# The last three bits of each converted weight: a GpSimd multiply-add in place of a ScalarE instruction

## The chip, the cores and the metric

One core of a Trainium2 chip. The metric is the device time of one execution in microseconds (us). Engines are named as the profile names them: PE is TensorE (matrix products; PEld its weight loads), DVE is VectorE, ACT is ScalarE, POOL is GpSimd, SP issues the DMAs.

## The reference

Attention with a memory, then two feed-forward blocks. The activations are float32; the feed-forward weights reach the device as 64-bit floats.

```python
scores = scale * q @ k.T                      # B, H, S, D = 4, 8, 576, 64; causal
a = softmax(scores); local = a @ v
mem_out = (phi(q) @ M_prev) / (phi(q) @ z_prev + 1e-06)
x = g * mem_out + (1 - g) * local             # -> [2304, 512]
x = ((x @ w1) * (x @ w2)) @ w3 @ w_out        # 512 -> 1024 -> 1024 -> 512
out = (sigmoid(x @ w_gate) * (x @ w_val)) @ w_out2   # 512 -> 1536 -> 512
```

## The kernel before

The kernel goes through the four batches in turn. While batch b is in its feed-forward part (`ffn`), the attention of batch b+1 is woven into it (`drive`, from line 1045). The time up to some 106 us is different: there the attention of batch 0 runs beside the preparation of a combined weight (w3 times w_out, `prep`, line 552; its products are the wps products of line 464). Attention works on four pairs of heads and, in each, on five row blocks of 116. For a pair p, a block i and a head hh of the pair the tile `p_<p>_<i>_<hh>` holds the scores. They go through TensorE (line 838, tile s), VectorE (line 843: mask, row maximum), ScalarE (line 119: exponential), VectorE (lines 866 and 867: reciprocal of the row sum), GpSimd or VectorE (line 869: scaling; in batch 0 always GpSimd), TensorE (line 899: transposes, tile t), and on to the products with the values (tile o). The memory part of a pair has two products that GpSimd may do (lines 781, tile me, and 790, tile mphi).

Every weight is a 64-bit float in memory. It is converted to a 32-bit float on the device, in halves of a unit of 128x512 numbers, 76 halves in all; `conv_step` does this. `load64` (line 282) brings a raw half of 512 KB into one of three buffers (tile r). Step 0 makes two tiles: cy on ScalarE (line 310) from the upper words, and cr (line 311) from the lower words, a whole number from 0 to 7 for the last three bits; both have two buffers. Behind step 0 the load of the half three places later is issued, and it waits until both instructions have read the buffer. Step 1 joins them on VectorE (line 319: cy shifted left by three, or cr) into the tile wraw. Then `split_step` splits the 32-bit number into two parts for TensorE's products: a cast on ScalarE (line 548) and a subtraction on VectorE (line 550) into the tile wo or wslot, which has five buffers. The function `pump` calls a conversion step and a split step between groups of products; while weights are missing, `prep` calls them directly.

The order on the engines: SP's opening and, from the first feed-forward on, TensorE's whole order are as the code writes them. All other orders are worked out when the kernel is built, by a scheduler that places each instruction by its own estimates of times and by priorities (the attention of batch 0 has a higher one). On the chip every engine goes through its list in that order, and an instruction that waits holds up all that stand behind it on its engine.

Of the kernel before, what the change touches and what calls it, by code (L numbers as in the profile page):

```python
# [10 lines left out]
U32 = mybir.dt.uint32  # L11
# [3 lines left out]
AF = mybir.ActivationFunctionType  # L15
ALU = mybir.AluOpType
# [35 lines left out]
HALF = 0.5 - 2.0**-12  # L52
LAST3 = 2.0**-29 * 7 / 8
# [9 lines left out]
def tile_attention_memory_ffn(  # L63
# [17 lines left out]
    nc = tc.nc  # L81
# [195 lines left out]
    def load64(n):  # L277
        if n < len(conv_slots):
            s = conv_slots[n]
            t = fp.tile([128, 512], I64, tag="r64", name=f"r64_{s}", bufs=R64)  # L280
            src = units[s // 2][0][s % 2]
            d = nc.sync.dma_start(out=t, in_=src.rearrange("p a c -> p (a c)"))
            raw64[s] = t
            last["dma"] = d

    def whole(u, hf):
        return raws[u][:, 4 * hf : 4 * hf + 4, :].rearrange("p a c -> p (a c)").bitcast(I32)

    def conv_step():
        s = ws["conv"]  # L290
        u, hf = divmod(s, 2)
        if u >= NU or (ws["step"] == 0 and ws["split"] < 2 * (u - 2)):
            return False
        src = units[u][0]
        if not isinstance(src, list):
            if not ws["wready"]:
                return False
            raws[u] = fp.tile([128, 8, 128], F32, tag="wraw", name=f"wraw{u}", bufs=3)
            last["dma"] = nc.sync.dma_start(out=raws[u], in_=src)
            ws["conv"] += 2  # L300
            return True
        if ws["step"] == 0:
            w = raw64.pop(s).bitcast(I32).rearrange("p (c two) -> p c two", two=2)
            y = fp.tile([128, 512], F32, tag="cy", name=f"cy{s}", bufs=2)
            r = fp.tile([128, 512], I32, tag="cr", name=f"cr{s}", bufs=2)
            hi = w[:, :, 1].bitcast(F32)

            nc.scalar.activation(out=y, in_=hi, func=AF.Prelu, scale=2.0**-112, alpha=2.0**32)  # L310
            nc.scalar.activation(out=r, in_=w[:, :, 0].bitcast(U32), func=AF.Copy, scale=LAST3, bias=HALF)
            load64(conv_rank[s] + R64)
            tmp["y"], tmp["r"] = y.bitcast(I32), r
            ws["step"] = 1
        elif ws["step"] == 1:
            if hf == 0:
                raws[u] = fp.tile([128, 8, 128], F32, tag="wraw", name=f"wraw{u}", bufs=3)
            y, z = tmp["y"], whole(u, hf)
            nc.vector.scalar_tensor_tensor(z, y, 3, tmp["r"], ALU.logical_shift_left, ALU.bitwise_or)  # L319
            if hf == 1 and u in kept:  # L320
                nc.sync.dma_start(out=kept[u], in_=raws[u])
            ws["step"] = 0
            ws["conv"] += 1
        return True
# [100 lines left out]
    def pump():  # L425
        late_scale()
        late_load()
        conv_step()
        split_step()
        ws["pumps"] += 1  # L430
        if phase["n"] == 2 and ws["pumps"] % 2 == 0:
            make_step()

    def need(store, s):
        while s not in store:
            moved = split_step()
            moved = conv_step() or moved
            ws["pumps"] += 1
            late_scale()
            late_load()  # L440
            assert moved
        return store[s]
# [109 lines left out]
    def prep(g):  # L552
        p, f0 = divmod(2 * g, F1)
        for m in range(4 * p, 4 * p + 4):
            while m not in wot:
                if not split_step():
                    conv_step()
                yield WAIT
# [622 lines left out]
```

## Time and profile before

| | |
|---|---|
| time, median of 3 runs (lowest, highest) | 1056.79 us (1052.53, 1061.76) |
| the profiled execution: time, span | 1057.47 us, 1055.7 us |
| PE, DVE, ACT, POOL busy in the span | 1024.9, 592.8, 557.4, 240.6 us |
| TensorE's granted clock, mean | 0.992 |
| bytes moved | 252.13 MB |

The span runs from the first to the last instruction; 1.8 us of the execution lie around it. TensorE's rows are modelled: its matmuls are pipelined, and a busy PE is not PE at its peak. Spans on POOL are rough. In the chain that ended last, each step goes back to what released an instruction, or to the one before it on its engine.

### The profile page before, as it was taken

To read this page: it belongs to the slowest core of one execution; us is meant where nothing else is said; L and a number is where in the kernel's file an instruction comes from. 1 tells how busy PE (TensorE), PEld (TensorE's weight loads), DVE (VectorE), ACT (ScalarE), POOL (GpSimd) and SP (SyncE) were. 2 spreads that over 40 slices of the span, in tenths; PEclk is the share of its full clock that TensorE was granted. 3 is DMA by queue.
4 is the path that set the end of the run, shared out by engine and by line. 5 is a ranking of instruction groups with operands and counts; after the bars stand their busy time and mean duration, and the time that the engine had idled before them with its cause. 6 is when DMAs were issued, how large, how long until landed. Compare 5 with 4: busy or idle time off the path is not lost.

```text
span 1055.7 us, 20138 instructions
## 1 busy us (share of the span) xinstructions
PE 1024.9 (97%) x7408; PEld 892.2 (85%) x7408; DVE 592.8 (56%) x1495; ACT 557.4 (53%) x1195; POOL 240.6 (23%) x238
## 2 busy tenths in 40 slices
PE   7999999999999999999999998999999999999998
PEld 3556778898999898889899895778999898899998
DVE  6655777666667468875655339654666311226620
ACT  7976787577767536555433435554544422234420
POOL 4354021212000112332233102332243100103420
PEclk9989999999999999999999999999999999999999
DMA  8665799878997598974788465413599444349971
GB/s 300 209 221 190 257 364 326 281 243 302 353 352 268 193 411 331 342 265 154 246 287 293 146 197 208 152 62 103 197 321 333 148 143 131 101 143 320 325 281 55
DMA packets 92667, 252.13 MB, mean 239 GB/s; under 512 B 11544, under 2 KB 30104, under 8 KB 92568
## 3 DMA queue, kind: packets, MB, share of 16 engines
q1 hardware_dynamic: 92568, 250.84, 68.7%
q8 instruction: 59, 0.97, 0.4%
q14 instruction: 40, 0.33, 0.1%
HBM read 186.31 MB, written 64.49 MB: 238 GB/s over the span
## 4 chain that ended last, share of the span: by engine, by line
PE 83%; DMA 6%; DVE 5%; ACT 3%; issue 1%; POOL 1%; SPq 0%; ACTq 0%; DVEq 0%; POOLq 0%
PE ab L464 17%; PE gvp L475 16%; PE ot L464 12%; PE xw L464 8%; PE gv L464 7%; PE s L838 6%; PE t L899 5%; PE wps L464 4%; PE o L967 4%; DMA wslot<-s 2%; PE o L952 2%; DMA wraw<-kf 1%; PE o L960 1%; DMA r<-in_gv_dram 1%; DVE p L843 1%
## 5 line engine op out<-in xcount | busy, mean ns | idle before, releaser
L464 PE MATMUL ab<-x,wslot 128*128 128x288 f32 (+1 forms) x1536 | 221.4, 297 | 0.8 <-ACT asb L617 0.8
L475 PE MATMUL gvp<-x,wslot 128*128 128x288 f32 x1512 | 204.9, 296 | 6.4 <-DMA wslot<-s 4.8
L475 PEld LDWEIGHTS gvp<-x,wslot 128*128 128x128 f32 x1512 | 202.0, 188 | 8.9 <-DVE hgraw L544 6.6
L464 PE MATMUL ot<-hg,wslot 128*128 128x288 f32 x1152 | 163.8, 298 | 1.2 <-DVE hg L550 1.2
L869 POOL TENSOR_SCALAR p<-p,sm,omg 116x116 f32<-116x116 f32 (+4 forms) x100 | 86.4, 869 | 336.5 <-DVE sm L867 247.3
L464 PEld LDWEIGHTS ot<-hg,wslot 128*128 128x128 f32 x1152 | 154.3, 188 | 7.5 <-issue 5.1
L119 ACT ACTIVATE p<-p,sm 116x116 f32<-116x116 f32 (+4 forms) x160 | 93.0, 583 | 59.7 <-DVE sm L843 59.4
L464 PEld LDWEIGHTS ab<-x,wslot 128*128 128x128 f32 x768 | 105.7, 191 | 8.6 <-issue 5.0
L464 PE MATMUL xw<-h,wslot 128*128 128x288 f32 x768 | 112.1, 299 | 0.5 <-POOL h L550 0.3
L464 PEld LDWEIGHTS xw<-h,wslot 128*128 128x128 f32 x768 | 103.3, 188 | 4.5 <-issue 2.5
L843 DVE CUSTOM_DVE_ANT_0 p<-s,msk 116x116 f32<-116x116 f32 (+4 forms) x160 | 68.2, 454 | 67.3 <-PE s L838 66.7
L464 PEld LDWEIGHTS <-wslot 128*128 128x128 f16 x768 | 73.8, 99 | 22.0 <-issue 3.1
L899 PE MATMUL t<-idf,p 116*116 116x116 f32 x480 | 69.1, 274 | 9.1 <-DVE sm L866 7.1
L464 PE MATMUL gv<-x,wslot 128*128 128x288 f32 x576 | 76.7, 295 | 0.6 <-ACT gsb L119 0.6
L464 PEld LDWEIGHTS gv<-x,wslot 128*128 128x128 f32 x576 | 76.4, 188 | 0.8 <-ACT gsb L119 0.8
L899 PEld LDWEIGHTS t<-idf,p 116*116 116x116 f32 x480 | 54.7, 140 | 23.5 <-ACT p L119 7.6
L550 DVE TENSOR_TENSOR wslot<-wraw,wslot 128x512 fp32r<-128x512 f32 x76 | 54.5, 719 | 34.1 <-ACT wslot L548 31.8
L622 DVE TENSOR_TENSOR hraw<-ab,asb 128x288 f32<-128x288 f32 x64 | 29.1, 454 | 57.8 <-PE ab L464 54.5
L310 ACT ACTIVATE cy<-r 128x512 f32<-128x512 f32 x76 | 51.5, 677 | 9.2 <-DVE wraw L319 2.0
L525 POOL TENSOR_TENSOR u4gv<-u2gv,s5gv 128x288 f32<-128x288 f32 x36 | 29.2, 812 | 117.4 <-ACT s5gv L523 75.1
L548 ACT CAST wslot<-wraw 128x512 fp32r<-128x512 f32 x76 | 47.2, 622 | 14.5 <-PE gv L464 4.2
L464 PE MATMUL wps<-wo,wslot 128*128 128x512 f32 x192 | 54.8, 422 | 0.0
(124 smaller groups left out, 1421.1 us busy)
## 6 DMA issues: line engine op xcount, KB each, us to landing
wslot<-k SPq DMA_DIRECT2D x112, 512.0 KB, 4.8
wslot<-s SPq DMA_DIRECT2D x72, 512.0 KB, 4.7
k<-wslot SPq DMA_DIRECT2D x48, 512.0 KB, 4.6
r<-in_gv_dram SPq DMA_DIRECT2D x24, 512.0 KB, 5.9
s<-wmade SPq DMA_DIRECT2D x24, 512.0 KB, 6.2
kf<-wraw SPq DMA_DIRECT2D x20, 512.0 KB, 4.2
qk<-in_qk_dram SPq DMA_DIRECT2D x32, 290.0 KB, 3.2
wslot<-k SPq DMA_DIRECT2D x36, 256.0 KB, 4.8
```

The costliest lines, as they stand in the source:

```text
L119: ins = nc.scalar.activation(**kw)
L310: nc.scalar.activation(out=y, in_=hi, func=AF.Prelu, scale=2.0**-112, alpha=2.0**32)
L464: nc.tensor.matmul(ps, w[:, wi, blk, :], x[:, xi, cols : cols + n], start=first and part == 0, stop=last and part == 2,)
L475: nc.tensor.matmul(ps, w[:, wi, blk + k, :], x[:, xi, k, :], start=k == 0 and part == 0, stop=k == 1 and part == 2,)
L525: nc.gpsimd.tensor_add(u4, u2, s5)
L548: nc.scalar.copy(dst[:, 0], src)
L550: eng.tensor_sub(dst[:, 1], src, dst[:, 0].bitcast(F32))
L838: nc.tensor.matmul(os_[hh], q_[r, 0, i * T : (i + 1) * T], k_[r, 1, c0:c1], start=x == 0, stop=x == len(terms) - 1,)
L843: nc.vector.tensor_tensor_reduce(out=ps_[hh][:, c0:c1], in0=os_[hh], in1=msk[:, SP - w + c0 : SP - w + c1], scale=-0.125, scalar=3.0e38 if ...
L869: lower(SHARE_N).tensor_scalar(ps_[hh][:, :w], ps_[hh][:, :w], sm[:, 6 + hh : 7 + hh], omg[:T, 2 * p + hh : 2 * p + hh + 1], ALU.mult, ALU ...
L899: nc.tensor.transpose(tp[:T, c : c + T], src[hh][:, j * T : (j + 1) * T], idf[:T, :T])
L967: nc.tensor.matmul(ot[r, XO + q0 : XO + S], v_[:, j, hh], pt[:, hh, j].rearrange("p a c -> p (a c)")[:, q0 - X : S - X] if j < 4 else pt[: ...
```

## The change

The tile cr is made by GpSimd, as one multiply-add with the same two constants, with unsigned integers in and integers out. Nothing else in the code is changed.

```diff
             nc.scalar.activation(out=y, in_=hi, func=AF.Prelu, scale=2.0**-112, alpha=2.0**32)
-            nc.scalar.activation(out=r, in_=w[:, :, 0].bitcast(U32), func=AF.Copy, scale=LAST3, bias=HALF)
+            nc.gpsimd.tensor_scalar(r, w[:, :, 0].bitcast(U32), LAST3, HALF, ALU.mult, ALU.add)
             load64(conv_rank[s] + R64)
```

Because the scheduler places the instructions, the other rows move too. On GpSimd, where the second head pair of batch 0 ends and the third begins (p_1_4_0 is the tile of pair 1, block 4, head 0; cr the new instruction, r the raw half, whose number is the one after r_; sm and omg are the factors of the scaling):

```order
 L869 TENSOR_SCALAR p_1_4_0_613<-p_1_4_0_613,sm_1_4_615,omg 116x580
 L869 TENSOR_SCALAR p_1_4_1_614<-p_1_4_1_614,sm_1_4_615,omg 116x580
+L311 TENSOR_SCALAR cr_1325<-r_18_1064 128x512
 L869 TENSOR_SCALAR p_2_0_0_665<-p_2_0_0_665,sm_2_0_667,omg 116x116
 L869 TENSOR_SCALAR p_2_0_1_666<-p_2_0_1_666,sm_2_0_667,omg 116x116
+L311 TENSOR_SCALAR cr_1342<-r_19_1140 128x512
 L781 TENSOR_TENSOR me_2_674<-mphi_2_675,z_2_651 116x640
 L869 TENSOR_SCALAR p_2_1_0_703<-p_2_1_0_703,sm_2_1_705,omg 116x232
```

Conversions 18 and 19 now stand between the scalings, ahead of the product me_2.

On ScalarE, the rows from the exponential of pair 1, block 3, head 1 to that of block 4, head 0, before (cy and cr are the two tiles of a conversion, r_12 the raw half 12):

```order
L119 ACTIVATE p_1_3_1_543,sm_1_3_544<-p_1_3_1_543,sm_1_3_544 116x464
L310 ACTIVATE cy_893<-r_12_701 128x512
L311 ACTIVATE cr_894<-r_12_701 128x512
L548 CAST x_0_599<-o_0_557 128x576
L119 ACTIVATE p_1_4_0_613,sm_1_4_615<-p_1_4_0_613,sm_1_4_615 116x580
```

And the same stretch now (pt are copies of transposed scores, wst a copy of a wps product, wslot a cast of a converted half):

```order
L119 ACTIVATE p_1_3_1_543,sm_1_3_544<-p_1_3_1_543,sm_1_3_544 116x464
L310 ACTIVATE cy_1060<-r_15_897 128x512
L548 CAST x_0_599<-o_0_557 128x576
L310 ACTIVATE cy_1136<-r_16_948 128x512
L310 ACTIVATE cy_1177<-r_17_1009 128x512
L917 COPY pt_1_241<-t_1_2_0_0_679 116x3x116
L917 COPY pt_1_241<-t_1_2_0_1_684 116x3x116
L572 COPY wst_728<-wps_1_605 128x512
L548 CAST wslot_794<-wraw_792 128x512
L119 ACTIVATE p_1_4_0_613,sm_1_4_615<-p_1_4_0_613,sm_1_4_615 116x580
```

The exponential of p_1_4_0 stood behind conversion 12 and stands behind conversion 17 now.

## Rows read from the trace of the kernel before

**Rows 1.** page, part 1: busy us, share of the span, instructions of each engine.
```profile
PE 1024.9 (97%) x7408; PEld 892.2 (85%) x7408; DVE 592.8 (56%) x1495; ACT 557.4 (53%) x1195; POOL 240.6 (23%) x238
```

**Rows 2.** busy us (instructions) of each engine by stage, then PEclk, DMA share, GB/s.
```profile
13.00:66.00 53.00, 51.37 (x211) 28.00 (x209) 40.38 (x126) 48.74 (x116) 24.40 (x28) 0.99 0.77 249
66.00:80.00 14.00, 14.00 (x53) 8.31 (x54) 5.28 (x19) 8.28 (x21) 6.15 (x8) 0.67 0.51 167
...
106.00:132.00 26.00, 24.37 (x143) 18.53 (x142) 19.27 (x44) 20.09 (x43) 1.85 (x3) 1.00 0.74 260
132.00:158.00 26.00, 25.68 (x165) 21.05 (x164) 19.28 (x48) 22.01 (x46) 6.24 (x5) 1.00 0.99 363
158.00:350.00 192.00, 189.18 (x1422) 174.22 (x1418) 126.80 (x279) 134.24 (x274) 21.71 (x20) 1.00 0.84 297
```

**Rows 3.** line 311 by source (ns min/median/max), by window (busy, count), and ScalarE's timeline.
```profile
L311 ACT ACTIVATE cr<-r x76: 642/666/734, 7.9 to 341.7; 128x512 int32<-128x512 uint32 x76
...
13.00:66.00 53.00, 11.53 (x17) 0.99 0.77 249
...
0.00:106.00 106.00, 14.93 (x22) 0.95 0.70 229
...
22.71 0.67 ACT L311 ACTIVATE cr<-r 128x512 int32<-128x512 uint32 x1
23.27 0.78 ACT L119 ACTIVATE p<-p,sm 116x580 f32<-116x580 f32 x1
```

**Rows 4.** chain that ended last, 0 to 66 us: by line, then start us, us, what.
```profile
by line: PE s L838 30.8%; PE t L899 13.8%; PE wps L464 13.8%; PE o L952 5.2%; DMA bt<-in_beta_dram 4.9%; PE o L967 4.8%; POOL p L869 4.2%; DVE p L843 3.6%; issue 3.0%; PE qt L926 2.7%; PE o L960 2.6%; POOL me L781 2.4%; ACT p L119 1.3%; DVE
...
32.44 4.99 PE wps L464 x11
...
57.29 1.11 POOL p L869 x2
...
58.91 1.64 POOL p L869 x2
...
60.83 1.56 POOL me L781
```

**Rows 5.** the same chain, 66 to 106 us.
```profile
73.11 2.85 PE o L967 x12
...
86.57 2.95 PE wps L464 x12
...
95.46 1.73 PE o L967 x12
```

**Rows 6.** the same chain, 106 to 350 us: first and last of four.
```profile
119.52 0.64 ACT cr L311
...
146.05 0.57 ACT cr L311
```

**Rows 7.** GpSimd by shape (busy us, mean ns, idle before), and line 869 by source.
```profile
L756 POOL TENSOR_TENSOR qkl<-qk,qkh 128x580 fp32r<-128x580 f32 x13 | 21.1, 1630 | 72.5 <-ACT qkh L755 45.5 <-PE t L899 20.8 <-DMA wslot<-k 6.1
L869 POOL TENSOR_SCALAR p<-p,sm,omg 116x580 f32<-116x580 f32 x20 | 20.2, 1015 | 37.1 <-DVE sm L867 23.0 <-PE ot L464 8.2 <-ACT cy L310 3.1
...
L869 POOL TENSOR_SCALAR p<-p,sm,omg x100: 436/832/1902, 7.5 to 844.2; 116x116 f32<-116x116 f32 x20, 116x232 f32<-116x232 f32 x20, 116x348 f32<-116x348 f32 x20, 116x464 f32<-116x464 f32 x20
```

**Rows 8.** line 319 by source; VectorE's and GpSimd's timelines near 16.5 us.
```profile
L319 DVE SCALAR_TENSOR_TENSOR wraw<-cy,cr x76: 629/684/1920, 8.6 to 348.5; 128x512 int32<-128x512 int32 x76
...
16.72 1.59 DVE L550 TENSOR_TENSOR wo<-wraw,wo 128x512 fp32r<-128x512 f32 x1
...
16.51 1.26 POOL L790 TENSOR_TENSOR mphi<-mphi,mn 116x640 f32<-116x640 f32 x1
```

**Rows 9.** the DMA queue's waits to 110 us (us, times, longest); DMA issues to 66 us.
```profile
SPq L282 <- ACT cr L311: 18.0, 12, 2.2
...
r<-in_w3t_dram SPq DMA_DIRECT2D x11, 512.0 KB, 4.5
```

## The prediction

> **What bounds the kernel now.** I read the page first, then the busy times by stage, the conversion's own line, the chain that ended last, GpSimd's instructions by shape, and the waits of the DMA queue. The page has TensorE busy for 97% of the span and ScalarE for 53% [rows 1], so an instruction taken off ScalarE is worth something only in a stretch where ScalarE ends last. The conversion's 76 instructions on line 311 start between 7.9 and 341.7 us [rows 3]; behind that the program is untouched, and I count nothing there.
>
> By stages [rows 2] the first 350 us differ. From 13 to 66 us (attention of batch 0, first conversions) ScalarE is busy 48.74 of 53 us, VectorE 40.38, GpSimd 24.40. From 66 to 80 us ScalarE has 8.28 of 14 and TensorE's granted clock is 0.67 of 2.4 GHz, so it spent much of it at 1.2; before it fell, TensorE had waited for VectorE and GpSimd (below). From 106 to 158 us ScalarE has 42.10 of 52, and TensorE stands idle for 1.63 + 0.32 = 1.95 us of it. So ScalarE is nearly full in one stretch only.
>
> The chain speaks against ScalarE even there. Over the first 66 us it gives ACT's largest line, the exponentials, 1.3%, and TensorE's s, t and wps products 30.8, 13.8 and 13.8% [rows 4]. Where the chain leaves TensorE in this stretch it goes to GpSimd: 1.11 and 1.64 us of line 869 and 1.56 us of line 781, between 57.29 and 62.39 us. TensorE's rows are modelled, so "busy" there may hide starving. That they were slow is not modelled away: eleven wps products from 32.44 us take 4.99 us, 454 ns each [rows 4], twelve from 86.57 us 2.95 us, 246 ns each [rows 5], although the clock column has 0.99 for 13 to 66 us [rows 2]. The chain is therefore one witness and the busy times of ScalarE the other, and they disagree. That is the open question of this prediction.
>
> **What is removed.** Line 311 takes 666 ns by the median [rows 3], but ScalarE overlaps its instructions: one starts at 22.71 us and the next at 23.27, so one instruction frees 0.56 us. 17 of them start between 13 and 66 us [rows 3]: 17 x 0.56 = 9.5 us freed of 48.74. If ScalarE were the bound all 9.5 would come back; by the chain none. What I do credit is the run of wps products at 32.44 us: it needs the first five weight halves, each of which passed this instruction, 5 x 0.56 = 2.8 us, and GpSimd now adds a step of its own to the same five. I take half, **-1.4 us**. Between 106 and 158 us four pieces of line 311 are on the chain, the first 0.64 and the last 0.57 us [rows 6], together some 2.4 us; TensorE idled 1.95 us there. It cannot win more than that; I take **-1.5 us**. From 158 to 350 us TensorE is busy 189.18 of 192 us [rows 2] and most of what is left is not this line's: 0.
>
> **What is added.** 76 GpSimd instructions of 128x512, unsigned integer in with every second word skipped, integer out, with one multiply and one add. The trace has no such form. From below: line 869, also two operations, takes 436 ns at the least; its 116x580 form has a mean of 1015 ns. From above: the two-input 128x580 form of line 756 takes 1630 ns [rows 7]. I take the nearest row, a one-input two-operation instruction of similar length: 1.0 us; the ends 0.44 and 1.63 stay for the range. GpSimd gets 17 x 1.0 us more between 13 and 66 us, 24.40 + 17 = 41.4 of 53.
>
> The Trainium skill (GPSIMD Engine Reference, Performance pitfalls for Q7 kernels) charges about 1.9 cycles per element up to an 8-byte step and 2.9 beyond. The step here is just 8 bytes. At its 1.2 GHz my estimate from that page is 0.81 us for 512 elements, and 1.24 us beyond the edge; by the first the term below would be 1.6 instead of 2.0 us. No row of this trace shows the form.
>
> Where the new instruction stands decides what it costs. At the place where the chain runs through GpSimd, two conversions (halves 18 and 19) now stand among the five instructions from p_1_4_0 to me_2, as the order shows. 2 x 1.0 = **+2.0 us** unless something later still holds that stretch. Behind them in GpSimd's queue are the normalisations of line 869 (TensorE's transposes wait for them) and the product of line 781 (VectorE's sum and, through it, TensorE wait).
>
> VectorE is the second cost. Line 319 takes 684 ns by the median and 1920 at the longest, and the subtraction of line 550 that starts at 16.72 us takes 1.59 us while GpSimd runs line 790 from 16.51 us [rows 8]: two-input VectorE work stretches by some 0.9 us when it meets GpSimd. Of 22 conversions before 106 us [rows 3] I let one in four do this where VectorE's own idle time (12.6 of 53 us in the full stretch) does not hide it, and of that a tenth reach TensorE: 22 / 4 x 0.9 x 0.1 = **+0.5 us**; bounds 0 and +5.
>
> The Trainium skill says why (SBUF — State Buffer, Who interferes with whom): an instruction of VectorE with two SBUF inputs and one of GpSimd that reads SBUF use the same port pair, and the later one waits for the whole of the earlier. By that rule the trace agrees (1.59 us against a median of 0.69), and this is the rule that speaks against the change. If every one of the 22 blocked VectorE to the end and nothing hid it, the term would be 20 us.
>
> **The wait that moves.** A load of the next raw half waits until its buffer is free: 12 waits on line 311, 18.0 us, stand in the DMA queue up to 110 us, and a load lands 4.5 us after issue [rows 9]. With three buffers a half can follow every (4.5 + 1.0 + about 1) / 3 = 2.2 us, against 53 / 17 = 3.1 us now. ScalarE's new order counts on that: the exponential p_1_4_0 stood behind conversion 12 and now stands behind conversion 17. If the halves do come faster this costs nothing, since the later stretch has fewer left; I set 0, and keep what it costs otherwise as a rival.
>
> **Sum.** -1.4 - 1.5 + 2.0 + 0.5 = -0.4 us on the profiled execution's 1057.47 us (span 1055.7 and 1.8 around it): 1057.1. The median of the runs is 0.7 us lower, so 1056.4; I forecast 1056.
>
> **Rivals.** *ScalarE was the bound.* TensorE's rows in the first 66 us hide starving. For it: 48.74 of 53 us busy, and products at half the later pace. Against it: the chain. Then 9.5 us come back, 1.95 us at 106 to 158, and TensorE, fed more densely, keeps its upper level through 66 to 80 us, where twelve o products took 2.85 us against 1.73 later [rows 5]; by that ratio ten slow microseconds give back about 4. GpSimd's and VectorE's +2.5 stay. From the median of 1056.8: 1056.8 - 9.5 - 1.95 - 4 + 2.5 = 1044 us.
>
> *GpSimd becomes the bound of the first stage.* The form costs 1.63 us, the halves come no faster than every 3.1 us, and the exponentials of the second head pair wait behind five conversions more. GpSimd would have 24.40 + 17 x 1.63 = 52.1 of 53 us: full. That is the point from which it decides; below some 1.3 us (46.5 of 53) it does not. Price: five halves at 3.1 - 2.2 us, 4.5 us, 2 x 1.63 = 3.3 at the GpSimd stretch, 2 from VectorE, and one more spell of TensorE at its lower level like that of 66 to 80 us, 4: with the 1.5 won behind 106 us, 1056.8 + 13.8 - 1.5 = 1069 us.
>
> **Chances and range.** The forecast's case, several small terms that cancel, 0.45; ScalarE the bound 0.27; GpSimd the bound 0.28. About 1%, 10.6 us, is what a measurement of this kernel can tell from no change, for its three runs lie 9 us apart. The first rival's 1044 is beyond 1% faster and the second's 1069 beyond 1% slower, so the chances are the same three. The likeliest case alone runs from 1048 (no cost at GpSimd, 4 us of ScalarE's time back) to 1064 (all of VectorE's +5 and the dearer form); to leave out no more than two in ten the range takes in both rivals' prices: 1041 to 1072.
>
> **What would show it.** Right: line 311 on GpSimd near 1.0 us; ScalarE between 13 and 66 us down to about 39 us and TensorE's s, t, wps still the chain there; the GpSimd pieces near 57 us on the chain longer by about 2 us; the gv products from 264 us at their old pace, and everything from 350 us on as long as before. Wrong to the fast side: the first wps run before 30 us and the clock whole between 60 and 80 us. Wrong to the slow side: line 311 above 1.3 us, GpSimd above 46 us in the first stage, or two-input VectorE lines with means above 0.9 us.

## The result, and the profile after

The changed kernel takes 1064.0 us (median of 16 runs, 1059.3 to 1072.65) against 1054.63 for the kernel before, timed beside it (16 runs, 1049.51 to 1061.76): ratio 1.0092, 95% interval 1.0074 to 1.0109. It is slower by 9.4 us. The prediction had said no change, 1056.

On the first part of the page of the changed kernel (columns as in [rows 1]) work has gone where the change sent it:

```profile
PE 1029.9 (97%) x7408; PEld 895.1 (84%) x7408; DVE 613.0 (58%) x1495; ACT 518.9 (49%) x1119; POOL 312.2 (29%) x314
```

ScalarE is 38.5 us lighter, GpSimd 71.6 heavier. By stages, with the columns of [rows 2]:

```profile
13.00:66.00 53.00, 50.26 (x194) 27.16 (x193) 37.79 (x99) 35.88 (x85) 36.39 (x39) 0.94 0.77 247
66.00:80.00 14.00, 11.49 (x56) 5.80 (x56) 11.23 (x38) 8.68 (x24) 9.82 (x12) 0.92 0.42 140
106.00:132.00 26.00, 24.34 (x127) 16.75 (x127) 17.25 (x38) 15.57 (x33) 8.12 (x9) 0.93 0.51 162
132.00:158.00 26.00, 25.08 (x166) 21.21 (x165) 20.84 (x50) 18.32 (x40) 12.09 (x13) 1.00 1.01 375
158.00:350.00 192.00, 191.35 (x1430) 175.42 (x1429) 139.33 (x282) 114.43 (x240) 61.85 (x61) 1.00 0.89 310
```

The counts in brackets are what to read here. From 13 to 66 us ScalarE is busy 12.9 us less, where 9.5 were expected: it gets through 85 instructions instead of 116, and only 17 of the 31 were taken off it. TensorE gets through 194 products instead of 211 and VectorE through 99 instructions instead of 126. Apart from TensorE, whose rows are modelled, no engine is near full over this stretch: VectorE has 37.79 and GpSimd 36.39 of 53 us. Work that is merely waiting does not show as busy.

Where the loss lies is read from the first start of a product that both kernels have. The products ab open the feed-forward part; the row of their line gives count, min/median/max in ns, and the first and last start in us, here of the kernel before:

```profile
L464 PE MATMUL ab<-x,wslot x1536: 283/290/448, 121.6 to 920.5; 128*128 128x288 f32 x96, 128*128 128x288 f16 x96
```

and of the changed kernel:

```profile
L464 PE MATMUL ab<-x,wslot x1536: 282/290/448, 133.3 to 928.0; 128*128 128x288 f32 x96, 128*128 128x288 f16 x96
```

The first ab comes 11.7 us late, the last 7.5. So in these two executions more than the whole loss has arisen by 133 us, and some 4 us come back later. The line itself, by source (ns min/median/max, first and last start; then what ended GpSimd's idle time before it, and who waited for it):

```profile
L311 POOL TENSOR_SCALAR cr<-r x76: 642/980/1177, 7.1 to 350.3; 128x512 int32<-128x512 uint32 x76
...
  DVE wraw L319: 84.7, 27
  DMA r<-in_wo_dram: 5.9, 1
...
  DVE wraw L319: 3.3, 5
```

Most of that idle time lies late, where it costs nothing (the experiments show it). Up to 110 us alone (busy us, mean ns, then the idle time before the instruction and its releasers):

```profile
L311 POOL TENSOR_SCALAR cr<-r 128x512 int32<-128x512 uint32 x22 | 16.8, 766 | 16.8 <-DMA r<-in_wo_dram 5.9 <-DVE wraw L319 5.3 <-DMA r<-in_w3t_dram 1.5
```

The median is what the prediction took, 1.0 us; in the first 110 us the instruction is shorter, 0.77 us. What is new is that GpSimd stands in front of it: for a buffer of cr that VectorE's line 319 frees, and for the raw half. 17 conversions start between 13 and 66 us, exactly as many as before: by then the halves have come no faster. What stands behind GpSimd meanwhile is seen in its timeline from 33 us (start us, us, instruction, and in brackets the idle time before it and what ended it):

```profile
33.59 1.40 POOL L311 TENSOR_SCALAR cr<-r 128x512 int32<-128x512 uint32 x2
36.34 0.78 POOL L311 TENSOR_SCALAR cr<-r 128x512 int32<-128x512 uint32 x1 [1.36 <-DVE mn L784]
38.66 0.67 POOL L311 TENSOR_SCALAR cr<-r 128x512 int32<-128x512 uint32 x1 [1.54 <-DMA r<-in_w3t_dram]
40.62 1.18 POOL L311 TENSOR_SCALAR cr<-r 128x512 int32<-128x512 uint32 x1 [1.30 <-DVE mn L786]
41.88 1.58 POOL L790 TENSOR_TENSOR mphi<-mphi,mn 116x640 f32<-116x640 f32 x1
43.45 2.01 POOL L869 TENSOR_SCALAR p<-p,sm,omg 116x232 f32<-116x232 f32 x2
...
62.85 1.65 POOL L869 TENSOR_SCALAR p<-p,sm,omg 116x580 f32<-116x580 f32 x2 [8.24 <-DVE sm L867]
```

Five conversions, three of them waiting, stand ahead of the product mphi and of the normalisation of the next row block. (A conversion takes nothing from mn; the two waits put down to mn end within 0.2 us of a line 319, which frees a buffer of cr.) The chain that ended last (start us, us, what) goes through just this place:

```profile
37.41 3.92 DMA r<-in_wo_dram
41.88 1.59 POOL mphi L790
43.52 1.22 PE qt L926 x5
...
80.33 4.77 PE wps L464 x12
```

A raw half lands, GpSimd converts it, then may do mphi, and TensorE's transposes qt wait for that, as TensorE's timeline has it:

```profile
43.52 1.22 PE L926 MATMUL qt<-idf,mphi 116*128 116x116 f32 x5 [2.27 <-POOL mphi L790]
```

Not all of the 3.92 us is the conversion's doing: mphi also takes mn, which VectorE finished at 40.62 us, where the conversion starts. The conversion itself held mphi from 40.62 to 41.88, for 1.26 us. Before, no conversion stood on GpSimd. In the last line twelve wps products take 4.77 us; twelve took 2.95 before [rows 5]. By the windows (columns as above) TensorE's granted clock is at its lower level, 0.5 of 2.4 GHz, from 45 to 50 us and again for most of 80 to 85; in the five microseconds ahead TensorE had stood idle for 2.31 and for 1.54 us:

```profile
40.00:45.00 5.00, 2.69 (x10) 1.39 (x9) 5.00 (x10) 3.79 (x9) 4.30 (x4) 0.86 0.68 189
45.00:50.00 5.00, 5.00 (x18) 2.06 (x17) 4.27 (x10) 3.33 (x10) 4.65 (x6) 0.50 0.81 267
75.00:80.00 5.00, 3.46 (x14) 2.36 (x14) 3.72 (x16) 1.80 (x7) 3.70 (x5) 0.77 0.05 18
80.00:85.00 5.00, 5.00 (x14) 3.70 (x12) 0.34 (x2) 3.19 (x8) 3.22 (x4) 0.55 0.37 119
```

The raw loads wait longer too. In the DMA queue's own waits to 110 us (us, times, longest) the 18.0 us of [rows 9] have become two rows, 32.8 us together:

```profile
SPq L282 <- ACT cy L310: 19.7, 15, 3.4
SPq L282 <- POOL cr L311: 13.1, 12, 3.1
```

### The profile page after: what moved, and what is told of

Same layout as the page of the kernel before. It is cut to its first block, busy times and chain, and to the rows that moved or that the text cites. A ratio compares the mean times of both kernels' runs of the same rounds, so it can differ in the third digit from the quotient of the medians.

```text
span 1063.2 us, 20248 instructions
## 1 busy us (share of the span) xinstructions
PE 1029.9 (97%) x7408; PEld 895.1 (84%) x7408; DVE 613.0 (58%) x1495; ACT 518.9 (49%) x1119; POOL 312.2 (29%) x314
## 4 chain that ended last, share of the span: by engine, by line
PE 82%; DVE 7%; DMA 4%; ACT 3%; issue 2%; POOL 1%; SPq 0%; DVEq 0%; POOLq 0%; ACTq 0%
PE ab L464 17%; PE gvp L475 16%; PE ot L464 13%; PE xw L464 10%; PE gv L464 7%; PE s L838 5%; PE t L899 4%; PE o L967 4%; PE wps L464 3%; DMA wslot<-s 2%; PE o L952 2%; DVE wraw L319 1%; PE o L960 1%; DVE p L843 1%; DVE wslot L550 1%
## 5 line engine op out<-in xcount | busy, mean ns | idle before, releaser
L869 POOL TENSOR_SCALAR p<-p,sm,omg 116x116 f32<-116x116 f32 (+4 forms) x100 | 90.7, 910 | 277.6 <-DVE sm L867 212.5
L311 POOL TENSOR_SCALAR cr<-r 128x512 int32<-128x512 uint32 x76 | 66.8, 880 | 105.4 <-DVE wraw L319 84.7
L550 DVE TENSOR_TENSOR wslot<-wraw,wslot 128x512 fp32r<-128x512 f32 x76 | 63.8, 840 | 37.5 <-ACT wslot L548 37.0
L319 DVE SCALAR_TENSOR_TENSOR wraw<-cy,cr 128x512 int32<-128x512 int32 x76 | 55.4, 757 | 5.5 <-POOL cr L311 3.3
```

The costliest lines, as they stand in the source:

```text
L311: nc.gpsimd.tensor_scalar(r, w[:, :, 0].bitcast(U32), LAST3, HALF, ALU.mult, ALU.add)
L550: eng.tensor_sub(dst[:, 1], src, dst[:, 0].bitcast(F32))
L869: lower(SHARE_N).tensor_scalar(ps_[hh][:, :w], ps_[hh][:, :w], sm[:, 6 + hh : 7 + hh], omg[:T, 2 * p + hh : 2 * p + hh + 1], ALU.mult, ALU ...
```

## The experiments

Every ratio is to the kernel before, timed beside the run. "First ab" is the first start of the ab products, read as above. The planner of the expectations is the scheduler.

### Which part of the change costs

**No instruction for the bits.** The tile cr is a constant zero, so the last three bits of every weight are left out.

```diff
-            nc.scalar.activation(out=r, in_=w[:, :, 0].bitcast(U32), func=AF.Copy, scale=LAST3, bias=HALF)
+            r = rz.to_broadcast([128, 512])
```

> Leaves out the last three bits of each converted weight: a constant zero stands in their place, so neither ScalarE nor GpSimd does anything for them. The instruction orders are again worked out at build time with a lighter ScalarE, and conversions stand ahead of the exponentials of batch 0 much as in the changed kernel (the exponential p_1_4_0 behind conversion 17). If the new order is what costs: slower than before by 4 to 12 us, first ab product near 127 to 133 us against 121.6. If GpSimd's instruction costs (VectorE blocked at the shared port, the scalings behind it in the queue): no slower than before, 1046 to 1055 us, first ab product at or ahead of 121.6 us.

Measured: 1046.26 us, ratio 0.9906 (0.987 to 0.9941); first ab at 117.1. On ScalarE and VectorE as many conversions stand ahead of the attention here as in the changed kernel (the exponential p_1_4_0 behind conversion 18 in both). So a lighter ScalarE, with the order that the scheduler makes of it, is worth 10 us, and that order by itself costs nothing. The exponential p_1_4_0 starts at 48.58 us in the kernel before, at 54.12 here and at 58.29 in the changed kernel: standing behind more conversions delays it in both, but only the changed kernel is slower for it.

**Both instructions.** GpSimd's instruction as in the change; ScalarE's old one stays too, and writes into cy, which is then overwritten.

```diff
+            nc.scalar.activation(out=y.bitcast(I32), in_=w[:, :, 0].bitcast(U32), func=AF.Copy, scale=LAST3, bias=HALF)
             nc.scalar.activation(out=y, in_=hi, func=AF.Prelu, scale=2.0**-112, alpha=2.0**32)
-            nc.scalar.activation(out=r, in_=w[:, :, 0].bitcast(U32), func=AF.Copy, scale=LAST3, bias=HALF)
+            nc.gpsimd.tensor_scalar(r, w[:, :, 0].bitcast(U32), LAST3, HALF, ALU.mult, ALU.add)
```

> The changed kernel, with the old ScalarE instruction kept as well (its result is overwritten), so ScalarE's load and with it the order stay near those of before (p_1_4_0 behind about 11 conversions), while GpSimd does its 76 instructions. If the new order costs: within 3 us of before. If GpSimd's instruction costs: as slow as the changed kernel or slower, +9 us or more.

Measured: 1052.79 us, ratio 0.9973 (0.9953 to 0.9993). By its own expectation this run speaks for the order as the cause, as the run before spoke for the instruction. The GpSimd instructions don't cost in every setting: here ScalarE has more to do for each half, and the scheduler puts fewer of them ahead of the attention.

**By the place in time.** The first 22 halves on ScalarE and the rest on GpSimd, and the other way round.

```diff
+            if conv_rank[s] >= 22:
+                nc.gpsimd.tensor_scalar(r, w[:, :, 0].bitcast(U32), LAST3, HALF, ALU.mult, ALU.add)
+            else:
                 nc.scalar.activation(out=r, in_=w[:, :, 0].bitcast(U32), func=AF.Copy, scale=LAST3, bias=HALF)
```

> The first 22 halves on ScalarE as before, the other 54 on GpSimd. All orders up to the last conversion before 106 us are those of before. Both theories put the loss ahead of 106 us: the first ab product near 121.6 us as before, and behind it the changed kernel's gain of some 4 us (its lag fell from 11.7 us at the first ab product to 7.5 at the last ot product): 1050 to 1052 us against 1054.6, so faster by 0.2 to 0.5%.

> The other way round: the first 22 halves on GpSimd, the other 54 on ScalarE. Both theories put the whole loss here: first ab product near 133 us, and no gain behind it: +10 to +13 us.

Measured: 1051.58 us, ratio 0.9966 (0.9942 to 0.9989), with the late ones on GpSimd; 1068.98, ratio 1.0133 (1.0098 to 1.0169), with the early ones. The first ab comes at 120.9 and at 138.2 us, the second some 5 us later than expected. The whole loss lies in the first 22 halves; the other 54 are no loss. In the second kernel's window TensorE does 167 products and has the lower clock for much of the time:

```profile
13.00:66.00 53.00, 46.83 (x167) 24.39 (x167) 35.66 (x90) 32.82 (x76) 34.50 (x37) 0.77 0.73 235
```

### What about the instruction costs

Three kernels keep ScalarE's and VectorE's place of conversions against the attention as in the first experiment, and give GpSimd something else to do for each half; the last three bits are left out in all of them.

```diff
-            nc.gpsimd.tensor_scalar(r, w[:, :, 0].bitcast(U32), LAST3, HALF, ALU.mult, ALU.add)
+            nc.gpsimd.tensor_scalar(r, zu.to_broadcast([128, 512]), LAST3, HALF, ALU.mult, ALU.add)
```

```diff
-            nc.gpsimd.tensor_scalar(r, w[:, :, 0].bitcast(U32), LAST3, HALF, ALU.mult, ALU.add)
+            nc.gpsimd.memset(r, 0)
```

In the third kernel, which has the second's fill, the tile r is one column:

```diff
-            r = fp.tile([128, 512], I32, tag="cr", name=f"cr{s}", bufs=2)
+            r = cp.tile([128, 1], I32, tag="cr1", name=f"cr{s}", bufs=2)
```

> The GpSimd instruction reads one constant per partition, spread over 512 columns, in place of the raw half: the last three bits are left out, the instruction keeps its length, its reading and its writing, and loses the wait for the raw load. ScalarE's and VectorE's orders are those of e1_no_bits (1046). Theory 'waits for raw loads stand in GpSimd's line': 1045-1050. Theory 'GpSimd's own time in front of the attention's steps' or 'GpSimd and VectorE get into each other's way when both read and write': 1058-1066, as after. Theory 'GpSimd's line is held by the two cr buffers, which VectorE frees': 1058-1066 too.

> GpSimd only writes zeros into cr (128x512, no operand read); last three bits left out, orders of all three engines as in e5_const_read. Raw loads: 1045-1050. GpSimd's own time: between 1046 and 1064 by the duration of the fill against 0.88 us. Engines in each other's way through reading: 1045-1050, well under e5_const_read. Line held by the cr buffers: 1058-1066.

> As e6_memset, but cr is one column per partition (128x1, two buffers) that VectorE reads spread out: the same 76 GpSimd instructions at the same places with the same buffer waits, each next to nothing long. Line held by the cr buffers: 1058-1066 still. GpSimd's own time, raw loads, or engines in each other's way: 1045-1050.

Measured: 1069.03 us, ratio 1.0126 (1.0092 to 1.0159); 1047.69, 0.9937 (0.9917 to 0.9957); 1046.78, 0.9926 (0.9905 to 0.9948). GpSimd's groups of the first 110 us (busy us, mean ns, idle time before and its releasers) of the first, the second and the third kernel:

```profile
L312 POOL TENSOR_SCALAR cr<-zu 128x512 int32<-128x512 uint32 x22 | 19.5, 886 | 12.6 <-DVE wraw L320 9.4 <-DVE sm L867 1.1 <-DVE sm L868 0.8
```

```profile
L311 POOL MEMSET cr<- 128x512 int32 x24 | 12.3, 525 | 13.4 <-DVE wraw L319 13.2
```

```profile
L311 POOL MEMSET cr<- 128x1 int32 x24 | 2.1, 98 | 18.6 <-DVE wraw L319 18.6
```

The third waits longest for its buffers and is as fast as the second: waiting for the two buffers of cr, alone, is not the loss. The first has no raw half to wait for and is at least as slow as the change: nor is the raw load, alone. 886 against 525 ns, 22 x 0.36 = 8 us of GpSimd's time, goes with 21 us of the kernel's, and the longer instruction also reads, where the fill only writes. But the scheduler knows these durations too, and TensorE's order changed with them: in the first of the three, as in the changed kernel, the transposes of the second head pair's last row block begin before the third pair's second row block of scores is complete; in the other two they begin within its third. So duration and order are not apart yet.

**GpSimd's order as written.** The changed kernel, with GpSimd's order in the first stage as the code issues it.

```diff
-    drive(start(), chain(a0, atts[1]), 42.4 * NPREP + 8 * WAIT, ATOT, 1.0, most=9)
+    with tc.manual_schedule(engines={mybir.EngineType.Pool}):
+        drive(start(), chain(a0, atts[1]), 42.4 * NPREP + 8 * WAIT, ATOT, 1.0, most=9)
```

> The changed kernel, nothing left out, with GpSimd's order of the first stage kept as the code issues it: normalisation of the second head pair's last row block behind conversion 9 instead of 18 (ScalarE's exponential of it behind 11 instead of 18, VectorE's row block behind 9 instead of 16). Theories that put the loss on the place of conversions in the line ahead of the attention (loads or buffers): 1046-1056. Theories that put it on GpSimd's work as such (own time, getting in VectorE's way): 1060-1066 as after, since the work is the same.

Measured: 1064.5 us, ratio 1.0102 (1.007 to 1.0134). A miss for every theory of "too many conversions ahead of the attention": with half as many ahead, the loss is the same. The conversions now come late instead: VectorE's line 319 waits for them 10.9 us to 110 us, where it waited 3.2 in the changed kernel. The loss has moved, too: the first ab comes at 123.3 us, only 1.7 us late, but the last of the wps products, the preparation of the combined weight, starts at 185.6 us against 176.6 before. The first ab alone is not a safe mark of where the loss arises.

### The order held fixed

The same edit, for TensorE, ScalarE, VectorE and GpSimd at once. In the first stage, to some 130 us, the order of these kernels is the same whatever an instruction takes; behind it the scheduler orders all but TensorE again.

```diff
+    with tc.manual_schedule(engines={mybir.EngineType.Pool, mybir.EngineType.Activation, mybir.EngineType.DVE, mybir.EngineType.PE}):
```

> The kernel before, with the orders of TensorE, ScalarE, VectorE and GpSimd in the first stage (the four head pairs of batch 0 and the first products of wo) kept as the code issues them, so that no duration that the planner assumes can move an instruction. The base of the next three. Both theories: no forecast of its own distance to before; 1045-1080.

> The changed kernel in the same fixed order as e9_fixed_before; only the instruction for the last three bits is on another engine. Theory 'GpSimd's own time, in front of the attention's steps on it, is the loss': slower than e9_fixed_before by 5 to 15 us, and slower than e11_fixed_tiny by 10 to 20. Theory 'the loss is the order that the planner makes of the changed durations': no slower than e9_fixed_before, rather faster by 2 to 10, as ScalarE has less to do.

> e7_tiny in the same fixed order (last three bits left out; GpSimd writes one column per half). GpSimd's own time: 10 to 20 us under e10_fixed_after. Order of the planner: within 4 us of e10_fixed_after.

> e5_const_read in the same fixed order (last three bits left out; GpSimd's instruction keeps its length but does not wait for the raw half). GpSimd's own time: within 4 us of e10_fixed_after. Waits for raw loads in GpSimd's line: near e11_fixed_tiny, under e10_fixed_after by the larger part of their difference. Order of the planner: within 4 us of both.

Measured: 1079.62 us, ratio 1.0252 (1.0234 to 1.027), for the kernel before; 1089.25, 1.034 (1.0314 to 1.0365), for the changed one; 1077.07, 1.0232 (1.0207 to 1.0257), with the tiny instruction; 1081.98, 1.0288 (1.0259 to 1.0318), without the wait for the raw half. With the first stage in one and the same order the change costs 9.6 us, as it does in the scheduler's (9.4). In the profiled executions 4.2 us of lag are there at the first ab (143.2 and 147.4 us), about where the fixed order ends, and 8.4 at the last wps product (199.2 and 207.6). That no reordering is needed is shown by the three kernels with a GpSimd instruction: their orders on VectorE, ScalarE and GpSimd are the same to the end, but for one fill at the start. Of the 12.2 us between the real instruction and the tiny one, 4.9 come with its length and its reading, which these runs don't separate, and 7.3 with taking the raw half, which it must wait for and whose buffer it holds. GpSimd's own time as the whole cause had been expected to leave the run without that wait within 4 us of the changed one; it is 7.3 under it. VectorE's lines 319 and 550 for the weights take 34.9 us up to 145 us in the kernel before and 36.3 in the changed one, 46 instructions in both, so VectorE working slower beside GpSimd explains little of it.

In this order a lighter ScalarE is worth 2.6 us (1079.62 to 1077.07), against 8 to 10 where the scheduler can use it.

How it costs is seen by following one place. TensorE's timeline at its first wps product, in the kernel before with this order and in the changed one:

```profile
30.11 1.80 PE L899 MATMUL t<-idf,p 116*116 116x116 f32 x8
36.12 0.80 PE L464 MATMUL wps<-wo,wslot 128*128 128x512 f32 x1 [4.22 <-ACT wslot L548]
```

```profile
30.54 1.80 PE L899 MATMUL t<-idf,p 116*116 116x116 f32 x8
41.03 0.80 PE L464 MATMUL wps<-wo,wslot 128*128 128x512 f32 x1 [8.69 <-ACT wslot L548]
```

The weight comes 4.9 us later. Back along its path, VectorE's timeline of the changed kernel at the two joins ahead of it:

```profile
31.95 0.69 DVE L319 SCALAR_TENSOR_TENSOR wraw<-cy,cr 128x512 int32<-128x512 int32 x1 [2.10 <-POOL cr L311]
...
39.63 0.69 DVE L319 SCALAR_TENSOR_TENSOR wraw<-cy,cr 128x512 int32<-128x512 int32 x1 [3.48 <-POOL cr L311]
```

and GpSimd's timeline of the same kernel, where the tile they wait for is made:

```profile
29.23 1.95 POOL L869 TENSOR_SCALAR p<-p,sm,omg 116x580 f32<-116x580 f32 x2 [5.56 <-DVE sm L867]
31.26 0.65 POOL L311 TENSOR_SCALAR cr<-r 128x512 int32<-128x512 uint32 x1
33.09 2.02 POOL L869 TENSOR_SCALAR p<-p,sm,omg 116x116 f32<-116x116 f32 x2 [1.18 <-DVE sm L867]
36.32 1.05 POOL L869 TENSOR_SCALAR p<-p,sm,omg 116x232 f32<-116x232 f32 x2 [1.22 <-ACT cy L310]
37.34 1.53 POOL L781 TENSOR_TENSOR me<-mphi,z 116x640 f32<-116x640 f32 x1
38.96 2.62 POOL L311 TENSOR_SCALAR cr<-r 128x512 int32<-128x512 uint32 x3
```

The conversion takes 0.65 us. But GpSimd first waits 5.56 us for VectorE's sm, the softmax's row sums, then normalises 1.95 us, and only then converts; the next three halves stand behind three such pieces of the attention. VectorE waits for the halves, and on VectorE the attention's own steps stand behind that wait. In the changed kernel's own order the line blocks the other way round as well: mphi and a normalisation behind conversions.

### The line without the normalisations

The fixed pair and the scheduler's pair again, with the normalisations of batch 0 (line 869) and line 790 on VectorE.

```diff
-SHARE_N = (1.0, 0.5, 0.5, 0.5)
-SHARE_M = (1.0, 0.3, 0.5, 0.5)
+SHARE_N = (0.0, 0.5, 0.5, 0.5)
+SHARE_M = (0.0, 0.3, 0.5, 0.5)
```

> e9_fixed_before with the normalisations of batch 0 (L869) and the scaling of q (L790) on VectorE, so that GpSimd has only the four products L781 of the attention in the first stage. The base of the next run; VectorE gets some 40 instructions more: 1075-1105.

> The changed kernel with the same two edits: against e13_fixed_before_norm only the instruction for the last three bits is on another engine. Theory 'one line': conversions and normalisations stand in each other's way because GpSimd takes both in order, so each half waits for the attention's softmax and the other way round; without the normalisations there the change costs nothing: -5 to +3 us against e13_fixed_before_norm. Theory 'the instruction itself': it is longer than ScalarE's and slows VectorE beside it, whatever else GpSimd has: +6 to +12, as between e9_fixed_before and e10_fixed_after (+9.6).

> The kernel before, in the planner's own order, with batch 0's normalisations (L869) and the scaling of q (L790) on VectorE. The base of the next run: 1060-1085, by VectorE's additional instructions.

> The changed kernel with the same two edits. Theory 'one line': the change's loss (+9.4 us between after and before) goes where GpSimd no longer has the normalisations: -10 to +4 against e17_before_norm. Theory 'the instruction itself': +6 to +12 against it.

Measured, fixed order: 1089.32 us, ratio 1.0337 (1.0305 to 1.037), before, and 1092.61, 1.037 (1.0338 to 1.0401), after. The change costs 3.3 us instead of 9.6, and these two intervals overlap, though the runs themselves do not (1087.4 to 1091.28 and 1091.99 to 1093.78); in the profiled executions the first ab even comes earlier with the change, at 150.4 against 154.2 us. Measured, the scheduler's order: 1058.3 us, ratio 1.0033 (1.0001 to 1.0066), and 1063.17, 1.0088 (1.0058 to 1.0117). The change costs 4.9 us instead of 9.4. Both results lie between the two forecasts.

Where the rest arises can be read from the profiled executions. The table has the starts of the last wps product and of the first ot product (the last product of the first batch's feed-forward part; the last conversion starts within 6 us behind it), without and with the change:

| pair | last wps, us | first ot, us | whole kernel, medians |
|---|---|---|---|
| scheduler's order | 176.6, 188.0: +11.4 | 335.9, 345.9: +10.0 | +9.4 |
| first stage fixed | 199.2, 207.6: +8.4 | 361.4, 368.4: +7.0 | +9.6 |
| first stage fixed, without the normalisations | 209.1, 209.2: +0.1 | 371.1, 370.4: -0.7 | +3.3 |
| scheduler's order, without the normalisations | 178.9, 183.5: +4.6 | 338.3, 341.4: +3.1 | +4.9 |

In the fixed order nothing of the change's loss is left by the first ot product once the normalisations are off GpSimd; the 3.3 us arise behind it, where hardly anything is converted any more. In the scheduler's order about two thirds of it go. So the line that conversions and attention share on GpSimd carries the loss in the one order and the larger part of it in the other. One execution stands for each kernel here, and executions of one kernel differ by some us. What the 3.1 us are that stay in the scheduler's order was not traced; one reservation is that VectorE has more to do in these kernels, which can change what a late half is worth.

### Fewer conversions on GpSimd

Every second of the first 22 halves on GpSimd, with all later ones; and the kernel with the first 22 on ScalarE once more.

```diff
-            if conv_rank[s] >= 22:
+            if conv_rank[s] >= 22 or conv_rank[s] % 2 == 1:
```

> e3_late_on_pool, and of the first 22 halves every second one on GpSimd too. Theory 'one line': the line is half as full, the loss of the first stage under half of the changed kernel's: 1050-1058. Theory 'the instruction itself': half of the loss: 1055-1060. Faster than e3_late_on_pool (1051.6) by either theory only if ScalarE's relief outweighs it.

> The kernel of e3_late_on_pool again, with five rounds: it was under both kernels, but by no more than 0.3%. Both theories: 1050-1053.

Measured: 1057.64 us, ratio 1.0026 (0.999 to 1.0061), for the half: the loss shrinks, and both theories had said so. 1050.77, ratio 0.9975 (0.9947 to 1.0003), for the late ones: with the first timing of the same kernel (0.9966) it is some 0.3% under the kernel before, the second time not clear of no change, and clearly under the changed kernel. That is the best version found that computes the whole result, and as an improvement it is hardly more than its uncertainty.

## Why the prediction was wrong

**The duration was near.** The line was taken at 1.0 us; it has a median of 0.98, a mean of 0.88 (66.8 us by 76), and 0.77 in the first 110 us, where the loss arises. ScalarE from 13 to 66 us was to fall to about 39 us and fell to 35.88, for it also got through less.

**The step that failed is the wait that moves, set at 0.** The text saw that the exponentials would stand behind more conversions and took the halves to come faster, from the time of the load ring alone (2.2 against 3.1 us a half). It took a half as ready when the instruction has run, and left out that GpSimd must first come to it. The halves came no faster over the stretch: 17 conversions in 53 us as before, 3.1 us a half, and with no instruction at all 19. (They ran ahead for a while: VectorE ended the join of the fifteenth half at 49.9 us instead of 56.1, but that of the seventeenth at 67.0 and 67.1.) The exponential p_1_4_0, behind five conversions more, started at 58.29 us instead of 48.58. In the fixed order the wait showed as line 319 waiting 2.10 and 3.48 us for a 0.65 us instruction, and the change cost 9.6 us though no exponential had another place. The waits of the raw loads, which the text had at 18.0 us to 110 us, became 32.8 instead of fewer.

**The price at GpSimd, +2.0 us, was counted at one place and in busy time.** Two instructions near 57 us were charged. The conversions stand between the attention's steps from the first head pair on, and the price at such a place is not the instruction alone but also what it waits for and whom it keeps waiting: mphi was held for 1.26 us by one conversion, and in the fixed order 7.3 of 12.2 us came with taking the raw half.

**The nearest rival had the right direction and the wrong trigger.** "GpSimd becomes the bound of the first stage" gave 1069 us and was to decide from 1.3 us an instruction, or 46.5 us of busy time. The instruction stayed at 0.88 and GpSimd at 36.39 us, and a loss of 9.4 us came all the same: none of the three signs named for the slow side showed. Its further spells of TensorE at the lower clock are there, at 45, 80 and 115 us (0.50, 0.55 and 0.66 in five-microsecond windows), while the one that the kernel before has from 65 to 75 us is gone.

**That 1064.0 lies in the range, and at the end of the likeliest case, is luck.** By the prediction's own terms that case ends at 1056.4 - 2.0 - 4 = 1050 and at 1056.4 + 4.5 + 1.3 = 1062 us, not at 1048 and 1064, and it was made of small terms that cancel; the measured loss comes mainly from a wait that was set at nothing. Nor is 1% what can be told from no change: with 16 runs of each kernel the interval is 0.2% to either side, and 0.9% stands clear of it.

**ScalarE was worth more than the chain said.** The forecast credited 1.4 us for the first run of wps products; with no instruction at all in its place the kernel gains 10 us (1046.26), and with the tiny one in the fixed order, where the scheduler can't use the relief, 2.6. "ScalarE was the bound", at 1044, had 9.5 us for ScalarE's time, close to the 10; the 1.95 and 4 us that it added did not come on top. GpSimd's line used the relief up: the first wps product starts at 32.9 us instead of 29.6.

**The 1.5 us between 106 and 158 us** did not come there: from the first ab to the first xw product it is 99.8 us after and 100.1 before. Between the first and the last start of the gvp products (line 475; 505.1 to 1013.7 us before, 515.5 to 1021.1 after) 3 us were regained in code that the change does not touch. That stretch takes 503 to 509 us in all the kernels profiled here, so the 3 us say nothing of the change.

**VectorE, +0.5 us.** The slowing exists, but mostly late. In the first 110 us line 319 has a mean of 851 ns instead of 763, 1.8 us over 20 instructions, and line 550's subtraction into wslot 754 instead of 731; from 110 to 350 us the latter has 868 instead of 716. The subtraction into wslot over the first 350 us (busy us, mean ns, idle before) in the kernel before, the changed one, the one with the fill, and the one with the late halves on GpSimd:

```profile
L550 DVE TENSOR_TENSOR wslot<-wraw,wslot 128x512 fp32r<-128x512 f32 x71 | 50.9, 718 | 33.8 <-ACT wslot L548 31.4 <-DMA k<-wslot 2.1
```

```profile
L550 DVE TENSOR_TENSOR wslot<-wraw,wslot 128x512 fp32r<-128x512 f32 x68 | 57.8, 851 | 35.4 <-ACT wslot L548 34.9
```

```profile
L550 DVE TENSOR_TENSOR wslot<-wraw,wslot 128x512 fp32r<-128x512 f32 x72 | 52.1, 726 | 41.4 <-ACT wslot L548 36.7 <-DMA kf<-wraw 4.2
```

```profile
L553 DVE TENSOR_TENSOR wslot<-wraw,wslot 128x512 fp32r<-128x512 f32 x71 | 59.7, 843 | 35.3 <-ACT wslot L551 34.8 <-DMA k<-wslot 0.3
```

Some 0.13 us each where GpSimd reads while VectorE works, none where it only writes. The last kernel has the full slowing and is not slower than before, so behind 106 us it costs nothing here.

## What to carry over

Before an instruction goes to an engine with time to spare, read what stands ahead of it there and what that waits for: on an engine that works in order, the work that is moved inherits every wait of its new neighbours, and they inherit its own. An engine that is two thirds busy can hold a kernel up, and a count of its busy time does not show it; the waits of whoever consumes the result do. Test it by holding the order fixed and swapping the moved instruction for a tiny one at the same place.

## What the runs showed of the hardware that was not expected

A GpSimd instruction that only writes SBUF (the 128x512 fill, 0.53 us) leaves VectorE's two-input subtraction at 726 ns; one of the same shape that reads a single column besides puts it at 837 ns, and the real one at 851. The Trainium skill (SBUF — State Buffer, Who interferes with whom) names reading by GpSimd as the condition; these runs agree for line 550, with the price above; line 319, with two inputs too, went only from 732 to 759 ns in the changed kernel, and has 707 beside the one-column reader, so the price is not the same for every line. GpSimd's own instruction took 0.65 us where VectorE stood waiting for it, and up to 1.18 elsewhere.

TensorE's granted clock is at its lower level in the changed kernel for most of 45 to 50 us (0.50), of 80 to 85 (0.55) and of 115 to 120 (0.66). Each time TensorE had stood idle before: for 2.31 us of 40 to 45, mostly one wait of 2.27 us for GpSimd's mphi; for 1.54 us of 75 to 80, in waits for VectorE's row maxima (0.36 and 1.19 us); and for 1.57 us of 110 to 115, in one wait for GpSimd's line 869. The kernel before has one longer spell, 0.50 from 65 to 75 us, after 1.58 us of idle time in 60 to 65. Idle time alone does not bring it: in the changed kernel in fixed order TensorE stood idle for 8.69 us ahead of 41.03 us, and the granted clock is 1.00 from 35 to 50.
